# Second attention batch's value products in plain float32, a later landing time in the load planner, and conversion buffers reused for kept weight parts

## The chip, the cores and the metric

The kernel runs on one core of one Trainium2 chip. The metric is the device time of one execution in microseconds (us). Before the change three runs gave 1292.48, 1296.36 and 1309.52 us, a median of 1296.36 us.

## The reference

Attention over 4 batches of 12 heads, 448 positions and 64 values a head, with q and k normalised by their root mean square; then two feed-forward nets on the 1792 tokens (768 to 2048 to 768), the first with a squared ReLU, the second with a PReLU. All in float32.

```python
def _attn_ref(q, k, v, g_q, g_k):
    q_n, k_n = (rmsnorm(q, g_q), rmsnorm(k, g_k))
    scores = scale * np.matmul(q_n, k_n.transpose(0, 1, 3, 2))
    scores = scores - np.max(scores, axis=-1, keepdims=True)
    attn = np.exp(scores)
    attn = attn / (np.sum(attn, axis=-1, keepdims=True) + 1e-09)
    return np.matmul(attn, v).astype(np.float32)
...
    h = np.maximum(x @ w_in, 0.0)
    return (h * h @ w_out).astype(np.float32)
...
    h = x @ w_in
    g = np.maximum(h, 0.0) + alpha * np.minimum(h, 0.0)
    return (g @ w_out).astype(np.float32)
```

## The kernel before, in words

**Numbers in two parts.** Most products on TensorE are not done in plain float32 but in float32r, with each factor split into a high part (a rounded copy) and a low part (the remainder, `rest`, L259). One product of two split factors is three matmuls: high by low, high by high, low by high. The helper `copy` (L248) makes high parts on ScalarE, VectorE or GpSimd, `rest` low parts on VectorE or GpSimd.

**Stages.** `with_attention` (L422) holds the attention of all four batches and the first net (`mlp`, kind 0) of batches 0 and 1, one batch at a time. `without` (L826) then runs the first net of batches 2 and 3 together and the second net of all, two batches at a time.

**Attention.** A batch has six pairs of heads. For a pair, `spread` (L628) makes two matmuls on TensorE (L636) that bring the norms into the layout of q and k, and VectorE multiplies (L641); there are 12 such matmuls a batch, 48 in all, and their rows mark how far attention has come. `prep` (L663) splits the result into parts (tiles mv and st). `shift` (L679) computes rough scores (L685) of which VectorE takes the row maxima (L689); a transpose (L692), a negated copy (L695) and a small DMA (L697) bring them into mv. `head` (L699) computes the scores (L710) in four blocks of keys, ScalarE takes exponentials (L718), and the values are multiplied in. This last step has two forms. Where (batch, pair) is in `IN_PARTS` (L23), v is split into vhl, blocks have 128 keys (the last 64), ScalarE takes each exponential twice, once rounded into tile hl and once in full, VectorE makes the remainder (L744, a call of `rest`), and TensorE does 3 + 3 + 3 + 2 float32r matmuls a head (L753). Where it isn't, blocks have 112 keys, ScalarE writes one float32 exponential into tile pf, and TensorE does four float32 matmuls a head (L729), each of which the trace shows as two records. `norm` (L760) divides and splits the result into xs.

**Weights.** They come in parts (`weight`, L265): 32 of the first matrix of a net, of 384 KB, and 24 of the second, of 512 KB. In batch 0's net the first net's weights arrive as raw float64 words: a load into one of three raw tiles, ScalarE (L292) and four VectorE steps (L294, L297, L301, L304) that make float32 in one of three ws tiles, then a high part by ScalarE and a low part by GpSimd in one of three whl tiles, and a store of whl to DRAM ("kept"). I call these steps one conversion; there are 56 in this stage. Batch 1's net, and the first net in `without`, load kept parts straight into whl. The second net's weights are converted in `without` in the same way.

**Order.** All engines run lists that are fixed when the kernel is built. `Tasks.run` (L99) makes them: each piece of work is a task with an urgency, prices in us for the engines that may do it, and dependencies; the scheduler plays it through and emits the task that can start soonest, by urgency where several can. Buffers come from named pools, and a task that needs one gets the one that comes free first by the plan. A load is planned (L161 and L162) to cost its bytes at a rate (`load`, L209) one after another, with a latency ahead of it and one behind. All DMAs are issued in one list by SyncE (SP), in order; one that waits keeps back those behind it.

Of the kernel before, what the change touches and what calls it, by code (L numbers as in the profile page):

```python
# [19 lines left out]
DM, DFF = 768, 2048  # L20
KD, KF = DM // 128, DFF // 128

IN_PARTS = {(b, p) for b in (2, 3) for p in range(NP)} | {(1, 3), (1, 4), (1, 5)}  # L23
GROUPS = ((2, 4), (2, 4))
SPARE = (("mv", 2), ("st", 2))
NSEL = max(max(g) for g in GROUPS)
# [26 lines left out]
class Tasks:  # L53
# [45 lines left out]
    def run(self):  # L99
        ready = {e: [] for e in self.ends}  # L100

        def offer(t):
            for e in t.on:
                ready[e].append(t)

        for t in self.new:
            for d in (*t.deps, *t.behind):
                if d.start is None:
                    t.missing += 1
                    d.next.append(t)  # L110
        for t in self.new:
            if not t.missing:
                offer(t)
        left = len(self.new)
        self.new = []
        while left:
            best = None
            for e, tasks in ready.items():
                found, soonest = [], None
                for t in tasks:  # L120
                    s = self.ends[e] + (max(t.gap, self.gap[e]) if e in "AV" else 0)
                    s = max(s, self.port) if e in t.alone else s
                    for d in t.deps:
                        s = max(s, d.end + (0 if d.engine == e == "T" else self.WAIT[e]))
                    for d in t.behind:
                        s = max(s, d.start)
                    taken = []
                    for b in t.bufs:
                        if b.ap is None:
                            taken.append(self.slot(b, taken))  # L130
                            s = max(s, taken[-1][0] + self.WAIT[e]) if taken[-1] else None
                            if s is None:
                                break
                    if s is None:
                        continue
                    if len(t.on) > 1:
                        other = min(max(self.ends[o], s, self.port if o in t.alone else 0) + self.PRICE[o] * t.on[o]
                                    + 0.7 * sum(x.on[o] for x in ready[o] if x.urgency < t.urgency)
                                    for o in t.on if o != e)
                        if s + self.PRICE[e] * t.on[e] > other + 0.2:  # L140
                            continue
                    found.append((s, t.urgency, t))
                    soonest = s if soonest is None else min(soonest, s)
                if found:
                    s, _, t = min((x for x in found if x[0] <= soonest + 0.05), key=lambda x: x[1])
                    if best is None or s < best[0]:
                        best = (s, e, t)
            assert best, "no task can start"
            s, e, t = best
            for o in t.on:  # L150
                ready[o].remove(t)
            for b in t.bufs:
                if b.ap is None:
                    _, n, b.pool = self.slot(b)
                    slots = self.free[b.pool]
                    b.slot = slots.pop(next(i for i, x in enumerate(slots) if x[1] == n))
                    b.ap = b.slot[2]
            t.engine, t.start = e, s
            if e == "S" and t.on[e]:
                self.ends[e] = s + 0.06  # L160
                self.dma = max(self.dma, s + 1.3) + t.on[e]  # L161
                t.end = self.dma + 0.8  # L162
            else:
                t.end = self.ends[e] = s + t.on[e]
                self.gap[e] = t.gap
                if e in t.alone:
                    self.port = t.end
            t.emit(e)
            left -= 1
            for b in t.bufs:  # L170
                b.left -= 1
                b.until = max(b.until, t.end)
                self.release(b)
            for n in t.next:
                n.missing -= 1
                if not n.missing:
                    offer(n)
# [15 lines left out]
def dve(n):  # L193
    return 0.07 + 0.00104 * n
# [12 lines left out]


def load(nbytes):  # L209
    return nbytes / 350e3  # L210


MM = 0.202
# [3 lines left out]
def attention_relu2_mlp_prelu_mlp(ctx: ExitStack, tc: tile.TileContext, qkt, qk_tm, v, gb, alpha, ident, sel,  # L217
# [18 lines left out]
    kept = {id(w1): [Buf(dram.tile([128, 2, UP], F32, name=f"w1_{i}")) for i in range(2 * KF)],  # L236
            id(w2): [Buf(dram.tile([128, 2, DN], F32, name=f"w2_{i}")) for i in range(4 * KD)]}
    y_dram = [[Buf(dram.tile([128, S], F32, name=f"y{b}_{d}")) for d in range(KD)] for b in range(2)]
    for name, n, dt, size in (("raw", 3, U32, 2 * DN), ("ws", 3, F32, DN), ("whl", 3, F32R, 2 * DN)):
        pooled(const, name, n, [128, size], dt)  # L240

    only = {}

# [21 lines left out]
    def weight(u, w, i, source, urgency, after):  # L265

        n = w.shape[-1] // 2
        both = Buf(pool="whl")
        parts = [(both, 0), (both, 1)]

        def part(k):
            return both.ap[:, k * n:k * n + n]

        def pair():
            return both.ap[:, :2 * n].bitcast(F32).rearrange("p (k n) -> p k n", k=2)

        if source == "kept":
            k = kept[id(w)][i]
            add(urgency, {"S": load(1024 * n)}, dma(pair, lambda: k.ap), [k], parts, "wh")
            return both  # L280
        raw, f = Buf(pool="raw"), Buf(pool="ws")
        add(urgency, {"S": load(1024 * n)}, dma(lambda: raw.ap[:, :2 * n], lambda: w[i]), [], [raw], "raw", after)

        def half(k):
            return raw.ap[:, :2 * n].rearrange("p (n two) -> p n two", two=2)[:, :, k]

        def fu():
            return f.ap[:, :n].bitcast(U32)


        add(urgency, {"A": act(n)},
            lambda e: nc.scalar.activation(out=f.ap[:, :n], in_=half(1).bitcast(F32), func=ACTF.Abs), [raw], [f], "f")  # L292
        add(urgency, {"V": dve2(n)},
            lambda e: nc.vector.tensor_scalar(out=f.ap[:, :n], in0=f.ap[:, :n], scalar1=TINY, scalar2=None, op0=ALU.max),  # L294
            [], [f])
        add(urgency, {"V": dve2(n)},
            lambda e: nc.vector.tensor_scalar(out=fu(), in0=fu(), scalar1=0x07FFFFFF, scalar2=3,  # L297
                                              op0=ALU.bitwise_and, op1=ALU.logical_shift_left), [], [f])

        add(urgency, {"V": dve(n)},  # L300
            lambda e: nc.vector.scalar_tensor_tensor(out=fu(), in0=half(1), scalar=0xC0000000, in1=fu(),  # L301
                                                     op0=ALU.bitwise_and, op1=ALU.bitwise_or), [raw], [f])
        add(urgency, {"V": dve(n)},
            lambda e: nc.vector.scalar_tensor_tensor(out=fu(), in0=half(0), scalar=29, in1=fu(),  # L304
                                                     op0=ALU.logical_shift_right, op1=ALU.bitwise_or), [raw], [f])
        add(urgency, on("wh", A=act(n), V=dve2(n)), lambda e: copy(e, part(0), f.ap[:, :n]), [f], [(both, 0)], "wh")
        add(urgency, on("wl", P=pool2(n), V=dve(n)), lambda e: rest(e, part(1), f.ap[:, :n], part(0)),
            [f, (both, 0)], [(both, 1)], "wl")
        if source == "first":
            k = kept[id(w)][i]  # L310
            add(urgency, {"S": load(1024 * n)}, dma(lambda: k.ap, pair), parts, [k], "keep")
        return both

    stream = []
    for s1, more in (("first", 0), ("kept", 0), ("kept", 2)):
        stream += [(w1, i, s1) for i in range(2 * KF)] + [(w2, i, s1) for i in range(4 * KD)]
        for _ in range(more):
            stream += [(w3, i, "f64") for i in range(2 * KF)] + [(w4, i, "f64") for i in range(4 * KD)]
    made, cur = {}, [0]

    def prepare(u, urgency, after=None):
        if u < len(stream) and u not in made:
# [99 lines left out]
    def with_attention():  # L422
        with ExitStack() as es:
# [378 lines left out]
            def give(bank):  # L802
# [3 lines left out]
                    ts.free["m"].append((bank.slot[0], bank.slot[1], bank.ap.rearrange("p (t n) -> p t n", t=1)))  # L806
                add(-100, {"S": 0}, emit, [], [bank], None, first_scores[0, H - 1])

            setup()
            attention(0, 0, True)  # L810
            for _ in range(2):
# [2 lines left out]
                prepare(u, 95, first_scores[0, 7])  # L814
            only.update(wl="P", wh="A")
            mlp(0, (0,), hg, to_dram(1, [y_dram[0]]), 10000, 140, 2.6)
            attention(1, 200)
            mlp(0, (1,), hg, to_dram(1, [y_dram[1]]), 20000, 340, 5.2)
            attention(2, 400)
            attention(3, 600)  # L820
            for u in range(cur[0], cur[0] + 3):
                prepare(u, 5000)
                made[u].open = True
            ts.run()

    def without():  # L826
        with ExitStack() as es:
            q1 = es.enter_context(tc.tile_pool(name="q1", bufs=1))
            pp = es.enter_context(tc.tile_pool(name="pp2", bufs=1, space=PSUM))
            hg = fixed(q1, [128, 2, KF, 2, S], F32R, "hg2")  # L830
            pooled(q1, "rl", 3, [128, 2, S], F32)
            pooled(q1, "y", 2, [128, 2, S], F32)
            pooled(pp, "m", 4, [128, 2, 512], F32)
# [83 lines left out]
```

## Time and profile before

| what | value |
|---|---|
| median of three runs | 1296.36 us |
| the profiled execution, its own time | 1297.45 us |
| its span, first to last instruction | 1295.6 us |
| TensorE, VectorE, ScalarE, GpSimd busy | 1232.6, 800.8, 720.9, 373.5 us |
| mean granted clock of TensorE | 0.978 of full speed |
| start of the last stage's products (m from xs) | 590.87 us |

The page of the profile gives busy times of the engines over the whole span and in 40 slices of 32.4 us. The view of stretches gives them between two points in time, with the granted clock and the busy share of the DMA engines. The chain that ended last lists, in order of time, which piece of work or which transfer the end hung on. The timeline lists an engine's instructions with the idle time ahead of them and what ended it. PE is TensorE, PEld its weight loads, DVE VectorE, ACT ScalarE, POOL GpSimd, SP or SPq SyncE's list of DMAs.

### The profile page before, as it was taken

The page shows a single profiled execution, that of the slowest core. Times are in us where ns is not written, and L with a number is a line of the kernel's source. Part 1 is how long each engine was busy: PE and PEld are TensorE (multiplying, and loading weights), DVE is VectorE, ACT ScalarE, POOL GpSimd, SP SyncE. Part 2 cuts the span into 40 slices and gives each one's busy share as a digit, 9 for nine tenths or more (in the row PEclk, how much of TensorE's full clock was granted, in tenths as well). Part 3 has the DMA queues.
Part 4 walks back from the last instruction along what each step waited for, and adds up shares of the span by engine and source line. Part 5 has one row for each costly group of instructions (what it writes and reads, how often), then busy time and mean ns, then how long its engine had stood idle before and what let it go on. Part 6 is the DMA issues. An engine that isn't in the chain of part 4 may idle for free.

```text
span 1295.6 us, 16918 instructions
## 1 busy us (share of the span) xinstructions
PE 1232.6 (95%) x5790; PEld 1073.4 (83%) x5790; DVE 800.8 (62%) x1419; ACT 720.9 (56%) x1350; POOL 373.5 (29%) x354
## 2 busy tenths in 40 slices
PE   4997899797999899999999999999999999999998
PEld 2556677675888788888999999999999999999997
DVE  6688899999888688602111000487895548786550
ACT  4788689776699879823333000366653336664331
POOL 3245345535345525310000000222232222223221
PEclk7998999998999899999999999999999999999999
DMA  5136658788445544257333323233354333334330
GB/s 184 54 117 228 237 202 277 275 280 274 170 145 180 193 145 136 81 188 246 105 105 120 114 100 112 83 105 111 125 180 155 119 114 98 114 123 137 133 112 29
DMA packets 69014, 194.45 MB, mean 150 GB/s; under 512 B 8320, under 2 KB 14592, under 8 KB 68928
## 3 DMA queue, kind: packets, MB, share of 16 engines
q1 hardware_dynamic: 68928, 193.38, 45.1%
q8 instruction: 45, 0.74, 0.2%
q14 instruction: 41, 0.34, 0.1%
HBM read 159.84 MB, written 33.42 MB: 149 GB/s over the span
## 4 chain that ended last, share of the span: by engine, by line
PE 80%; DVE 10%; ACT 4%; DMA 3%; issue 2%; SPq 0%; POOL 0%; ACTq 0%; DVEq 0%
PE m L343 54%; PE bank L343 11%; PE bank L710 5%; PE pv L753 4%; PE pv L729 3%; PE bank L685 2%; DVE mc L689 1%; DVE ws L301 1%; DMA whl<-w 1%; DVE hl L259 1%; DVE ws L304 1%; DVE ws L294 1%; DMA tm<-in_qk_tm 1%; DMA raw<-in_w 1%; DVE ss L588 1%
## 5 line engine op out<-in xcount | busy, mean ns | idle before, releaser
L259 POOL TENSOR_TENSOR whl<-ws,whl 128x384 fp32r<-128x384 f32 (+2 forms) x169 | 204.9, 1215 | 683.4 <-ACT whl L251 405.2
L343 PE MATMUL m<-xs,whl 128*128 128x448 f32 x1728 | 350.8, 365 | 0.7 <-ACT rl L251 0.7
L343 PE MATMUL m<-hg,whl 128*128 128x448 f32 x1728 | 350.7, 365 | 0.0
L343 PEld LDWEIGHTS m<-xs,whl 128*128 128x128 f32 x1728 | 324.5, 188 | 26.7 <-ACT rl L251 1.1
L343 PEld LDWEIGHTS m<-hg,whl 128*128 128x128 f32 x1728 | 324.5, 188 | 25.7
L292 ACT ACTIVATE ws<-raw 128x384 f32<-128x384 f32 (+1 forms) x168 | 101.3, 603 | 133.5 <-POOL whl L259 112.3
L294 DVE TENSOR_SCALAR ws<-ws 128x384 f32<-128x384 f32 (+1 forms) x168 | 68.0, 409 | 142.6 <-ACT ws L292 142.4
L343 PE MATMUL bank<-xs,whl 128*128 128x448 f32 x576 | 142.4, 382 | 7.8 <-POOL xs L259 3.3
L251 ACT ACTIVATE whl<-ws 128x384 fp32r<-128x384 f32 (+1 forms) x167 | 94.4, 566 | 77.3 <-PE m L343 57.1
L343 PE MATMUL bank<-hg,whl 128*128 128x448 f32 x576 | 130.6, 369 | 2.2 <-DMA whl<-w 2.2
L343 PEld LDWEIGHTS bank<-xs,whl 128*128 128x128 f32 x576 | 111.5, 196 | 21.2 <-POOL xs L259 3.7
L343 PEld LDWEIGHTS bank<-hg,whl 128*128 128x128 f32 x576 | 108.9, 191 | 11.8 <-DMA whl<-w 2.6
L304 DVE SCALAR_TENSOR_TENSOR ws<-raw,ws 128x384 uint32<-128x384 uint32 (+1 forms) x168 | 116.3, 698 | 2.7
L689 DVE TENSOR_REDUCE mc<-bank 112x1 f32<-112x448 f32 x192 | 110.3, 615 | 11.4 <-PE bank L685 10.2
L259 DVE TENSOR_TENSOR hg<-m,hg 128x896 fp32r<-128x896 f32 x48 | 52.1, 1086 | 94.1 <-ACT hg L251 93.6
L301 DVE SCALAR_TENSOR_TENSOR ws<-raw,ws 128x384 uint32<-128x384 uint32 (+1 forms) x168 | 106.5, 639 | 3.7
L710 PE MATMUL bank<-mv,st 128*128 128x448 f32 (+2 forms) x352 | 102.2, 397 | 5.3 <-ACT mn L695 2.4
L259 DVE TENSOR_TENSOR hl<-bank,hl 128x448 fp32r<-128x448 f32 (+1 forms) x120 | 73.7, 618 | 32.6 <-ACT bank L718 31.5
L753 PE MATMUL pv<-hl,vhl 128*128 128x448 f32 x330 | 87.3, 374 | 1.3 <-DVE hl L259 1.3
L685 PE MATMUL bank<-st,mv 128*112 128x448 f32 x176 | 62.2, 411 | 22.5 <-DVE mc L689 7.8
L710 PEld LDWEIGHTS bank<-mv,st 128*128 128x128 f32 (+2 forms) x352 | 60.9, 182 | 24.9 <-DVE mc L689 6.3
L297 DVE TENSOR_SCALAR ws<-ws 128x384 uint32<-128x384 uint32 (+1 forms) x168 | 72.7, 439 | 3.6
(110 smaller groups left out, 1259.5 us busy)
## 6 DMA issues: line engine op xcount, KB each, us to landing
raw<-in_w SPq DMA_DIRECT2D x96, 384.0 KB
raw<-in_w SPq DMA_DIRECT2D x72, 512.0 KB
whl<-w SPq DMA_DIRECT2D x64, 384.0 KB
whl<-w SPq DMA_DIRECT2D x48, 512.0 KB
w<-whl SPq DMA_DIRECT2D x32, 384.0 KB
w<-whl SPq DMA_DIRECT2D x24, 512.0 KB
qk<-in_qkt SPq DMA_DIRECT2D x24, 448.0 KB
tm<-in_qk_tm SPq DMA_DIRECT2D x40, 224.0 KB
```

The lines of the kernel that those rows point to most:

```text
L251: nc.scalar.activation(out=o, in_=i, func=ACTF.Copy)
L259: (nc.gpsimd if e == "P" else nc.vector).tensor_tensor(out=o, in0=x, in1=hi, op=ALU.subtract)
L292: lambda e: nc.scalar.activation(out=f.ap[:, :n], in_=half(1).bitcast(F32), func=ACTF.Abs), [raw], [f], "f")
L294: lambda e: nc.vector.tensor_scalar(out=f.ap[:, :n], in0=f.ap[:, :n], scalar1=TINY, scalar2=None, op0=ALU.max),
L297: lambda e: nc.vector.tensor_scalar(out=fu(), in0=fu(), scalar1=0x07FFFFFF, scalar2=3, op0=ALU.bitwise_and, op1=ALU.logical_shift_left), [ ...
L301: lambda e: nc.vector.scalar_tensor_tensor(out=fu(), in0=half(1), scalar=0xC0000000, in1=fu(), op0=ALU.bitwise_and, op1=ALU.bitwise_or), [ ...
L304: lambda e: nc.vector.scalar_tensor_tensor(out=fu(), in0=half(0), scalar=29, in1=fu(), op0=ALU.logical_shift_right, op1=ALU.bitwise_or), [ ...
L343: nc.tensor.matmul(out=acc.ap[:, t, :S], lhsT=w.ap[:, part * n + 128 * kk:part * n + 128 * kk + 128], rhs=src(h, k0 + kk, t)[1](), start=( ...
L685: lambda e, t=t, pm=pm: nc.tensor.matmul(out=pm.ap[:CP, :S], lhsT=m.ap[:, 0, t * CP:(t + 1) * CP], rhs=s.ap[:, 0, :], start=True, stop=Tru ...
L689: lambda e, t=t, pm=pm: nc.vector.reduce_max(out=mc.ap[:, t:t + 1], in_=pm.ap[:CP, :S], axis=AX.X),
L710: nc.tensor.matmul(out=pa.ap[:keys, :S], lhsT=s.ap[:rows, k, c:c + keys], rhs=m.ap[:rows, k, :], start=(k == 0), stop=(k == 1))
L753: nc.tensor.matmul(out=o.ap[:, :S], lhsT=l, rhs=r, start=(n == 0 and x == 0), stop=(half and x == 1))
```

## The change

**What it does.** Three edits. (1) `IN_PARTS` loses pairs 3, 4 and 5 of batch 1, so that all of batch 1's value products are plain float32, as batch 0's are (the host lays out v by the same set). (2) The planner counts 2.0 us ahead of a load and 1.4 us behind it, where it counted 1.3 and 0.8, and a rate of 320 GB/s where it counted 350. (3) raw and ws are no longer allocated for the whole kernel. In `with_attention` they lie in a pool of their own, which is closed behind the last conversion of that stage (`no_more`); four more tiles of whl's size, named more, take its room and serve as further buffers for kept parts until that stage ends. `without` allocates raw and ws anew.

```diff
-IN_PARTS = {(b, p) for b in (2, 3) for p in range(NP)} | {(1, 3), (1, 4), (1, 5)}
+IN_PARTS = {(b, p) for b in (2, 3) for p in range(NP)}
...
             if e == "S" and t.on[e]:
                 self.ends[e] = s + 0.06
-                self.dma = max(self.dma, s + 1.3) + t.on[e]
-                t.end = self.dma + 0.8
+                self.dma = max(self.dma, s + 2.0) + t.on[e]
+                t.end = self.dma + 1.4
...
 def load(nbytes):
-    return nbytes / 350e3
+    return nbytes / 320e3
...
-    for name, n, dt, size in (("raw", 3, U32, 2 * DN), ("ws", 3, F32, DN), ("whl", 3, F32R, 2 * DN)):
-        pooled(const, name, n, [128, size], dt)
+    pooled(const, "whl", 3, [128, 2 * DN], F32R)
+
+    def converting(pool):
+
+        pooled(pool, "raw", 3, [128, 2 * DN], U32)
+        pooled(pool, "ws", 3, [128, DN], F32)
...
-        both = Buf(pool="whl")
+        both = Buf(pool=("whl", "more") if "more" in ts.free else "whl")
...
-        add(urgency, on("wl", P=pool2(n), V=dve(n)), lambda e: rest(e, part(1), f.ap[:, :n], part(0)),
+        converted[0] = add(urgency, on("wl", P=pool2(n), V=dve(n)), lambda e: rest(e, part(1), f.ap[:, :n], part(0)),
...
+            wp = es.enter_context(ExitStack())
+            converting(wp.enter_context(tc.tile_pool(name="wp", bufs=1)))
+
+            def no_more():
+
+                def emit(e):
+                    until = max(x[0] for n in ("raw", "ws") for x in ts.free[n])
+                    wp.close()
+                    pool = wp.enter_context(tc.tile_pool(name="wq", bufs=1))
+                    ts.free["more"] += [(until, i, pool.tile([128, 2 * DN], F32R, name=f"more{i}")) for i in range(4)]
+
+                add(-100, {"S": 0}, emit, [], [], None, converted[0])
+
+            ts.pool("more", [])
             setup()
             attention(0, 0, True)
...
             mlp(0, (0,), hg, to_dram(1, [y_dram[0]]), 10000, 140, 2.6)
+            no_more()
             attention(1, 200)
...
             attention(3, 600)
+            del ts.free["more"]
             for u in range(cur[0], cur[0] + 3):
                 prepare(u, 5000)
                 made[u].open = True
+            ts.pool("more", [])
             ts.run()
+            del ts.free["more"]
...
             hg = fixed(q1, [128, 2, KF, 2, S], F32R, "hg2")
+            converting(q1)
```

**What it does to the order.** Since the scheduler plays all of this through, the order changes on every engine, from the first microseconds on. How many MLP products (L343) stand ahead of a spread matmul on TensorE, and how many conversions (L304) ahead of that spread's product on VectorE (L641):

| spread matmul | 13th (batch 1) | 17th | 21st | 25th (batch 2) | 29th | 33rd |
|---|---|---|---|---|---|---|
| MLP products before | 15 | 117 | 195 | 456 | 552 | 621 |
| MLP products now | 15 | 108 | 204 | 279 | 420 | 558 |
| conversions before | 5 | 17 | 26 | 48 | 56 | 56 |
| conversions now | 4 | 16 | 27 | 37 | 48 | 56 |

In the changed kernel the line numbers are 4 higher. VectorE where the values of pair 3 of batch 1 are multiplied, before: hg is a remainder of the net's hidden layer, hl one of the exponentials, mc the maxima of rough scores, ws a conversion.

```order
L259 TENSOR_TENSOR hl_175<-bank_150,hl_175 128x448
L689 TENSOR_REDUCE mc_185<-bank_154 112x1
L259 TENSOR_TENSOR mv_159<-bank_152,mv_159 64x448
L689 TENSOR_REDUCE mc_185<-bank_150 112x1
L689 TENSOR_REDUCE mc_185<-bank_154 112x1
L259 TENSOR_TENSOR hg<-bank_153,hg 128x448
L259 TENSOR_TENSOR hl_176<-bank_151,hl_176 128x448
L294 TENSOR_SCALAR ws_138<-ws_138 128x384
L294 TENSOR_SCALAR ws_136<-ws_136 128x384
```

And there now:

```order
L263 TENSOR_TENSOR hg<-bank_149,hg 128x448
L693 TENSOR_REDUCE mc_180<-bank_148 112x1
L305 SCALAR_TENSOR_TENSOR ws_195<-raw_193,ws_195 128x384
L298 TENSOR_SCALAR ws_196<-ws_196 128x384
L308 SCALAR_TENSOR_TENSOR ws_195<-raw_193,ws_195 128x384
L301 TENSOR_SCALAR ws_196<-ws_196 128x384
L693 TENSOR_REDUCE mc_180<-bank_145 112x1
L305 SCALAR_TENSOR_TENSOR ws_196<-raw_192,ws_196 128x384
L693 TENSOR_REDUCE mc_180<-bank_146 112x1
```

The hl remainders are gone, and conversions and maxima stand closer to each other.

SP around the loads of kept parts 18 to 22 of the first matrix (w1_18 to w1_22), in the stretch with batches 2 and 3, before: whl0 to whl2 are the three buffers, qk, tm and v attention's inputs.

```order
L262 DMA whl1_140<-w1_18_83 128x768
L262 DMA tm0_171<-in_qk_tm 112x512
L262 DMA tm1_172<-in_qk_tm 112x512
L262 DMA whl2_141<-w1_19_84 128x768
L262 DMA tm0_171<-in_qk_tm 112x512
L262 DMA whl0_139<-w1_20_85 128x768
L262 DMA qk0_166<-in_qkt 128x896
L262 DMA qk1_167<-in_qkt 128x896
L262 DMA whl1_140<-w1_21_86 128x768
L262 DMA tm1_172<-in_qk_tm 112x512
L262 DMA whl2_141<-w1_22_87 128x768
```

And now:

```order
L266 DMA more3_2924<-w1_18_83 128x768
L266 DMA qk1_161<-in_qkt 128x896
L266 DMA tm0_165<-in_qk_tm 112x512
L266 DMA v0_162<-in_v 128x768
L266 DMA whl2_135<-w1_19_84 128x768
L266 DMA tm1_166<-in_qk_tm 112x512
L266 DMA whl0_133<-w1_20_85 128x768
L266 DMA whl1_134<-w1_21_86 128x768
L266 DMA more0_2921<-w1_22_87 128x768
```

The same parts go through seven buffers in turn, so that a buffer's load waits for the part seven places back to be used, where it waited for the one three places back.

## Rows read from the trace of the kernel before

**Rows 1.** The page: busy time, then tenths in 40 slices.
```profile
PE 1232.6 (95%) x5790; PEld 1073.4 (83%) x5790; DVE 800.8 (62%) x1419; ACT 720.9 (56%) x1350; POOL 373.5 (29%) x354
...
PE   4997899797999899999999999999999999999998
...
DVE  6688899999888688602111000487895548786550
...
PEclk7998999998999899999999999999999999999999
```

**Rows 2.** Stretches: length, busy PE, PEld, DVE, ACT, POOL (instructions), clock, DMA share, GB/s.
```profile
300.00:325.00 25.00, 15.66 (x63) 12.50 (x62) 22.98 (x42) 14.72 (x28) 14.56 (x14) 0.80 0.75 262
...
442.50:451.84 9.34, 6.09 (x17) 5.39 (x18) 3.71 (x7) 5.35 (x12) 3.29 (x4) 0.63 0.63 215
...
556.00:590.87 34.87, 31.98 (x159) 29.05 (x157) 0.62 (x1) 5.09 (x9) 3.46 (x3) 1.00 0.63 208
590.87:1295.60 704.73, 700.68 (x3456) 649.02 (x3456) 340.02 (x552) 274.75 (x416) 130.47 (x112) 1.00 0.36 119
...
110.14:345.16 235.02, 203.75 (x886) 164.08 (x886) 217.96 (x424) 180.32 (x374) 104.36 (x90) 0.94 0.72 247
345.16:590.87 245.71, 238.58 (x1154) 208.30 (x1154) 162.03 (x285) 184.84 (x394) 94.51 (x96) 0.99 0.47 154
```

**Rows 3.** The chain that ended last: start us, us, what.
```profile
73.91 2.31 PE pv L729 x6
...
438.81 6.90 DMA whl<-w
...
568.48 6.96 DMA whl<-w
...
587.59 2.70 DMA whl<-w
590.87 700.70 PE m L343 x3456
```

**Rows 4.** TensorE's timeline: start us, us, instruction, [idle before, what ended it].
```profile
110.14 1.05 PE L636 MATMUL bank<-rhl,selg 128*128 128x448 f32 x4 [1.78 <-DVE rhl L259]
...
163.56 0.82 PE L636 MATMUL bank<-rhl,selg 128*128 128x448 f32 x2 [0.18 <-DVE rhl L259]
...
198.44 0.93 PE L636 MATMUL bank<-rhl,selg 128*128 128x448 f32 x2
...
317.51 0.69 PE L685 MATMUL bank<-st,mv 128*112 128x448 f32 x1 [6.24 <-ACT ws L292]
...
345.16 0.65 PE L636 MATMUL bank<-rhl,selg 128*128 128x448 f32 x2 [0.40 <-DVE rhl L259]
...
445.75 3.73 PE L343 MATMUL bank<-xs,whl 128*128 128x448 f32 x9 [3.26 <-DMA whl<-w]
...
575.49 0.68 PE L343 MATMUL bank<-hg,whl 128*128 128x448 f32 x2 [2.21 <-DMA whl<-w]
```

**Rows 5.** VectorE's groups, 110.14 to 345.16: count, busy us, mean ns, idle before.
```profile
L689 DVE TENSOR_REDUCE mc<-bank 112x1 f32<-112x448 f32 x64 | 37.4, 614 | 3.4 <-PE bank L685 3.0
L304 DVE SCALAR_TENSOR_TENSOR ws<-raw,ws 128x384 uint32<-128x384 uint32 (+1 forms) x52 | 31.9, 630 | 0.2
L301 DVE SCALAR_TENSOR_TENSOR ws<-raw,ws 128x384 uint32<-128x384 uint32 (+1 forms) x51 | 31.6, 637 | 0.1
L297 DVE TENSOR_SCALAR ws<-ws 128x384 uint32<-128x384 uint32 (+1 forms) x51 | 23.6, 481 | 0.1
L294 DVE TENSOR_SCALAR ws<-ws 128x384 f32<-128x384 f32 (+1 forms) x51 | 21.1, 429 | 4.5 <-ACT ws L292 4.2
L259 DVE TENSOR_TENSOR hl<-bank,hl 128x448 fp32r<-128x448 f32 (+1 forms) x30 | 17.9, 614 | 0.8 <-ACT bank L718 0.6
...
L259 DVE TENSOR_TENSOR st<-bank,st 64x448 fp32r<-64x448 f32 x16 | 10.0, 622 | 0.6 <-ACT st L251 0.2
...
L259 DVE TENSOR_TENSOR vhl<-v,vhl 128x768 fp32r<-128x768 f32 x1 | 2.0, 2047 | 0.0
```

More of the change, by code (lines that the diff above doesn't have):

```diff
@@ L318, in attention_relu2_mlp_prelu_mlp @@
             stream += [(w3, i, "f64") for i in range(2 * KF)] + [(w4, i, "f64") for i in range(4 * KD)]
-    made, cur = {}, [0]
+    made, cur, converted = {}, [0], [None]
     def prepare(u, urgency, after=None):
```

## The prediction

> **What bounds the kernel now.** I read the page's slices first [rows 1]: TensorE is busy for 95% of the span, so only its gaps and its slow-clock stretches can be had. From slice 19 on it stands at 9 with the granted clock at 9; before that it falls to 6 and 7, with the clock down to 7 and 8. The stretches [rows 2] put the border at 590.87 us: behind it 700.7 us of 704.7 are busy, and the chain [rows 3] holds nothing there but one piece of 700.70 us, 3456 products. That gives the price of a product that I use below, 700.70 / 3456 = 0.203 us. The change alters nothing that this stage computes, so its cost stays.
>
> The time to be had lies in the 590.87 us ahead. I cut it where the spread matmuls stand [rows 4], which mark how far attention has come: the 13th (first of batch 1) at 110.14 and the 29th (batch 2, second pair) at 345.16, just after the last weight conversion. In the first stretch, 110.14 to 345.16, VectorE is busy for 217.96 of 235.02 us (93%) and TensorE for 203.75 [rows 2]; what TensorE waits for there is VectorE work, as in front of the 317.51 us row, where it stood for 6.24 us [rows 4]. (The row names ScalarE's conversion; VectorE was doing that conversion's next steps.) So VectorE sets the pace. In the second stretch, to 590.87, VectorE is down to 162 of 246 us and TensorE at 239: TensorE sets it. What it loses there are mostly waits for kept weights: 3.26 us at 445.75, with a mean granted clock of 0.63 around it (part of that stretch at the lower of its two levels, 1.2 and 2.4 GHz), and 2.21 us at 575.49 [rows 2, 4].
>
> **Pairs 3 to 5 of batch 1 in float32.** Each of six heads loses 11 products (3+3+3+2) and gains four float32 products. Six records of L729 take 2.31 us in the chain [rows 3]; two records are one product, so 0.77 us. TensorE: 24 x 0.77 - 66 x 0.203 = +5.1 us. VectorE loses 24 subtractions of hl at some 0.61 us, ScalarE 24 exponentials, GpSimd and VectorE the split of three v tiles. These pairs lie in the first stretch (of its 30 hl rows on VectorE [rows 5], 24 are theirs and 6 batch 2's).
>
> A rule of the Trainium skill bears on the price: FP8 and Floating Point Precision, TensorE Precision Notes, counts four passes for true FP32. At 0.203 us a pass that would be 0.81 us and +6.1 in all; the row's 0.77 is taken here.
>
> What this does to the first stretch I work out from the orders. By VectorE's order the last conversion stands ahead of the 29th spread before, and ahead of the 33rd now: batch 1's attention has become cheaper, and the scheduler puts more attention, two pairs of batch 2, among the conversions. So I compare VectorE's work from the 13th spread to the 29th before with that from the 13th to the 33rd now, at its mean durations [rows 5]. Before it sums to 242 us, which with overlaps filled 218. Now: one conversion more (four steps, 0.63 + 0.64 + 0.48 + 0.43 = +2.2), 16 maxima (16 x 0.614 = +9.8), 12 spread products and mv and st remainders (12 x 0.62, st's row, = +7.5), 8 hl remainders fewer (-4.9), a v split fewer (-2.0), the small ones together -1.2: 253 us. At the same overlap and the same 93% that takes 253/242 x 235.0 = 246.0 us: the 33rd spread comes at 356.2.
>
> TensorE's work left behind that point now: 594 MLP products, 144 of scores, 64 of maxima, 206 of values, 16 spreads, all at 0.203, and 17 transposes of 0.1: some 209 us. Before, behind the 29th spread: 600, 176, 80, 250, 20 and 21, some 230 us, done in 245.7 us, a rate of 0.938. At that rate 209 us take 223.2, and the stretch ends at 579.4 instead of 590.9: **-11.5 us**, with the 5.1 us of float32 inside. ScalarE covers this: it is busy for 180 of 235 us in the first stretch and 185 of 246 in the second [rows 2], and has no more rows per pair than before.
>
> **Four more buffers for kept parts, and loads planned later.** The new tiles lie where raw and ws were, and their first loads stand behind the last conversion, as SP's order shows. From then on seven parts can be on their way or in store. Before, three: a load of 384 KB took 6.90 us in the chain, and at 568.48 one of 512 KB 6.96 [rows 3], while TensorE uses a part up in 9 x 0.203 = 1.8 or 12 x 0.203 = 2.4 us. Three parts in store cover 5.5 to 7.3 us, seven 12.8 to 17. Price: around 445.75 TensorE did 18 products, 3.6 us, in 9.34; in the last 34.87 us it did 159 by the records, 32.3 us [rows 2]. So 5.7 + 2.6 = 8.3 us are there to be had; nothing, at the other end, if SP still issues late. SP takes its DMAs in order, and loads of qk, tm and v that wait for VectorE stand among those of parts; with seven in store such a block is covered. I take **-6**.
>
> The planner counted 1.3 + 1.1 + 0.8 = 3.2 us for a 384 KB load and now counts 2.0 + 1.2 + 1.4 = 4.6. The rows show 6.90 and 2.70 [rows 3]; 4.6 lies between them. The Trainium skill speaks against this part: in DMA: Bandwidth & Descriptors, Anatomy of one DMA, a fit (for GpSimd's path) gives 2.0 us plus the bytes at 436 GB/s, 2.9 us here. By it the old plan was right and this edit is worth nothing; 6.90 us disagrees, 2.70 agrees. I give the plan no term of its own.
>
> In the third stage raw and ws are allocated anew, over tiles of attention's stage, so the first raw load waits in SP's queue for the last product on hg. Behind it stand loads of kept parts, which wait for TensorE to free a buffer anyway, with three parts loaded: 0 us. If that cover failed, one part's wait of 2.70 us [rows 3] would be the cost.
>
> **A held-back part.** Between the 17th and the 25th spread the new order leaves TensorE 171 MLP products where 339 stood, with the float32 products of batch 1 in between: 90 us of TensorE's work beside 99 of VectorE's, which at 0.90 overlap and 93% would take 96 us. Both engines close to full at once: from the 17th to the 21st before, 33.2 us of TensorE's work were done in 34.9 (163.56 to 198.44 [rows 4]), 0.95, but over the whole first stretch 184 in 235, 0.78. By the first nothing is lost, by the second 90/0.78 - 96 = 19. I take **+4**, nearer the first, since there too the work was balanced.
>
> **Sum.** -11.5 - 6 + 4 = -13.5. The profiled execution took 1297.45 us, 1295.6 of it span; 1.1 more than the median of 1296.36. So 1284 for it, and 1283 for a median.
>
> **The rivals.** *Nothing to gain (0.17).* The relief is eaten by the denser first stretch (+12 instead of +4) and the parts land no sooner, since SP's order is fixed and its blocks remain: the four buffers then don't do what they were put there for. -11.5 + 12 + 0: 1297. For it: ScalarE and DMA are also 72 to 77% busy there [rows 2]. Against it: neither is the one waited for longest.
>
> *The idle time of VectorE goes too (0.12).* Of its 17 us idle in the first stretch, half goes because raw parts are asked for earlier, and both waits for parts vanish: -11.5 - 8.3 - 8.5, or 1268. For it: 4.5 us of it are waits for ScalarE's first step [rows 5], which itself waits for raw loads. Against it: VectorE's waits are spread over many causes.
>
> *TensorE starves between the 17th and 25th spread (0.13).* With half the MLP products, heads wait for their own chain (maxima, transpose, a small DMA, exponentials), and TensorE's clock goes down with its gaps, as in the slice from 300 to 325 us: 15.66 of 25 busy at a clock of 0.80 [rows 2]. At a rate of 0.70 the 90 us take 129, 33 more than 96: -11.5 - 6 + 33 = +15.5, or 1312. It decides from a rate of 0.79 down, where the 17.5 us are used up. For it: the first stretch had just 0.78. Against it: VectorE was what held it down.
>
> **How the numbers follow.** The forecast, 1272 to 1293, has 0.58. The range of 1268 to 1299 takes in the second rival at its own figure and the first whole, and leaves out most of the third. A measurement of this kernel tells about 2%, 26 us, from no change: faster than 1270.4 is most of the second rival (0.10), slower than 1322 the end of the third (0.04), the rest, 0.86, lies within.
>
> **What would show it.** Right: the 33rd spread near 356 us with the conversions just done, VectorE at 93% up to there; the piece of 3456 products beginning near 577; no wait for whl or more over 1 us in TensorE's rows of the second stretch. Wrong: TensorE's busy time from the 17th to the 25th spread under 80% with VectorE under 90% (the third rival); a start of the last stage before 565 (the second); waits for kept parts as long as before (the first).

## The result and the profile after

The changed kernel takes 1275.38 us (median of four runs, 1274.14 to 1275.94) where the kernel before took 1294.43 (median of its four, with one more run than ahead of the prediction). The ratio is 0.9865, with a 95% interval of 0.9841 to 0.9889: faster by 1.35%. The forecast was 1283, with a range of 1268 to 1299. Single late executions pull a ratio, so below the median stands beside it where the two differ.

The stretches of the changed kernel, cut at the same marks as in [rows 2]: the first, its part from the 17th to the 25th spread matmul, the second, the last stage. Columns as there.

```profile
111.18:352.44 241.26, 223.28 (x973) 175.29 (x974) 228.38 (x446) 196.37 (x411) 129.10 (x101) 0.97 0.72 247
352.44:567.41 214.97, 213.67 (x1050) 188.64 (x1048) 136.10 (x240) 158.73 (x336) 79.88 (x81) 1.00 0.54 171
156.81:252.40 95.59, 93.07 (x380) 66.17 (x380) 89.51 (x177) 84.48 (x181) 53.09 (x44) 1.00 0.71 238
567.41:1272.40 704.99, 700.87 (x3456) 649.72 (x3456) 340.71 (x552) 274.17 (x416) 129.85 (x112) 1.00 0.38 119
```

TensorE's timeline at the marks, which answer to [rows 4]:

```profile
111.18 1.08 PE L640 MATMUL bank<-rhl,selg 128*128 128x448 f32 x4 [2.50 <-DVE rhl L263]
...
252.40 1.34 PE L640 MATMUL bank<-rhl,selg 128*128 128x448 f32 x4
...
352.44 0.57 PE L640 MATMUL bank<-rhl,selg 128*128 128x448 f32 x2
...
567.41 8.78 PE L347 MATMUL m<-xs,whl 128*128 128x448 f32 x42 [0.68 <-ACT rl L255]
```

The chain that ended last, at the border that [rows 3] show at 590.87:

```profile
527.04 39.70 PE bank L347 x195
...
567.41 700.88 PE m L347 x3456
```

The 33rd spread stands at 352.44 us (forecast: 356), the last stage begins at 567.41 (forecast: 577) instead of 590.87 and costs the same 705 us, and ahead of it 195 products run in one piece of 39.70 us (0.204 us each) where the chain of [rows 3] passes through two loads of kept parts. The two executions profiled are 23 us apart; the medians, 19. The profiled execution of before is 3 us above its median, and its stretch of 235.02 us [rows 2] was shorter in others, as the runs below show.

### The profile page after: what moved, and what is told of

Same layout as the page of the kernel before. It is cut to its first block, busy times and chain, and to the rows that moved or that the text cites. A ratio compares the mean times of both kernels' runs of the same rounds, so it can differ in the third digit from the quotient of the medians.

```text
span 1272.4 us, 16814 instructions
## 1 busy us (share of the span) xinstructions
PE 1227.0 (96%) x5772; PEld 1065.8 (84%) x5772; DVE 781.9 (61%) x1390; ACT 708.1 (56%) x1326; POOL 387.0 (30%) x353
## 4 chain that ended last, share of the span: by engine, by line
PE 79%; DVE 10%; ACT 6%; issue 2%; POOL 1%; DMA 1%; SPq 0%; ACTq 0%; POOLq 0%; DVEq 0%
PE m L347 55%; PE bank L347 11%; PE bank L714 4%; PE pv L757 3%; PE pv L733 3%; PE bank L689 2%; DVE mc L693 2%; DVE ws L305 1%; DVE ws L308 1%; DMA tm<-in_qk_tm 1%; DVE bank L645 1%; DVE ws L298 1%; DVE ss L592 1%; ACT mv L255 1%; DVE st L263 1%
## 5 line engine op out<-in xcount | busy, mean ns | idle before, releaser
L263 POOL TENSOR_TENSOR whl<-ws,whl 128x384 fp32r<-128x384 f32 (+2 forms) x169 | 209.5, 1242 | 668.1 <-ACT whl L255 375.4
L305 DVE SCALAR_TENSOR_TENSOR ws<-raw,ws 128x384 uint32<-128x384 uint32 (+1 forms) x168 | 105.0, 628 | 3.9
L347 PE MATMUL bank<-xs,whl 128*128 128x448 f32 x405 | 100.5, 380 | 5.5 <-POOL xs L263 5.2
L714 PE MATMUL bank<-mv,st 128*112 128x448 f32 (+2 forms) x352 | 98.4, 390 | 0.7 <-ACT pf L722 0.5
L347 PE MATMUL bank<-hg,whl 128*128 128x448 f32 x420 | 93.4, 367 | 0.0
L347 PEld LDWEIGHTS bank<-xs,whl 128*128 128x128 f32 x405 | 77.5, 194 | 15.9 <-POOL xs L263 5.6
L347 PEld LDWEIGHTS bank<-hg,whl 128*128 128x128 f32 x420 | 79.2, 190 | 6.4
L301 DVE TENSOR_SCALAR ws<-ws 128x384 uint32<-128x384 uint32 (+1 forms) x168 | 73.7, 443 | 3.8
L263 DVE TENSOR_TENSOR hl<-bank,hl 128x448 fp32r<-128x448 f32 (+1 forms) x96 | 59.1, 620 | 27.3 <-ACT bank L722 24.3
L714 PEld LDWEIGHTS bank<-mv,st 128*112 128x112 f32 (+2 forms) x352 | 60.1, 178 | 18.6 <-issue 4.4
L689 PE MATMUL bank<-st,mv 128*112 128x448 f32 x176 | 62.9, 414 | 12.1 <-DVE st L263 9.4
L757 PE MATMUL pv<-hl,vhl 128*128 128x448 f32 x264 | 69.0, 370 | 1.9 <-DVE hl L263 1.6
```

Of the source, the lines that this page charges most:

```text
L263: (nc.gpsimd if e == "P" else nc.vector).tensor_tensor(out=o, in0=x, in1=hi, op=ALU.subtract)
L347: nc.tensor.matmul(out=acc.ap[:, t, :S], lhsT=w.ap[:, part * n + 128 * kk:part * n + 128 * kk + 128], rhs=src(h, k0 + kk, t)[1](), start=( ...
L689: lambda e, t=t, pm=pm: nc.tensor.matmul(out=pm.ap[:CP, :S], lhsT=m.ap[:, 0, t * CP:(t + 1) * CP], rhs=s.ap[:, 0, :], start=True, stop=Tru ...
L714: nc.tensor.matmul(out=pa.ap[:keys, :S], lhsT=s.ap[:rows, k, c:c + keys], rhs=m.ap[:rows, k, :], start=(k == 0), stop=(k == 1))
L757: nc.tensor.matmul(out=o.ap[:, :S], lhsT=l, rhs=r, start=(n == 0 and x == 0), stop=(half and x == 1))
```

## The experiments

All ratios are to the kernel before on the same chip. The three edits were tried alone and in pairs, then the pace of the first stretch.

**Edit 1 alone.**

```diff
-IN_PARTS = {(b, p) for b in (2, 3) for p in range(NP)} | {(1, 3), (1, 4), (1, 5)}
+IN_PARTS = {(b, p) for b in (2, 3) for p in range(NP)}
```

> Edit 1 alone (batch 1's values all in plain float32; planner and buffers as before). Theory, VectorE's relief: the 33rd spread comes near 356 us as in the forecast, the waits for kept parts stay (3 us near 445, 2 us near 575), the whole is 9 to 12 us shorter than before (ratio 0.991 to 0.993). Rival, the later planned landing is what shortens the first stretch: within 3 us of before. Rival, TensorE starves between the 17th and 25th spread: slower than before by 5 us or more.

Measured: 0.9967 (0.9941 to 0.9993), 4 us; 6 by the medians. The 33rd spread came at 364.69 us, not at 356, and in the stretch up to it ScalarE waited 12.9 us for raw parts. The view of stretches, 13th to 33rd spread, then the view of waits there (who <- for whom: us in total, times, longest):

```profile
110.81:364.69 253.88, 225.80 (x971) 178.07 (x971) 231.37 (x444) 194.54 (x403) 122.78 (x107) 0.96 0.71 238
```

```profile
ACT ws L292 <- DMA raw<-in_w: 12.9, 11, 4.3
```

So a third to a half of the forecast's 11.5 us came out. The waits for kept parts stayed, but none over 0.7 us: that part of the expectation fell.

**Edit 2 alone.**

```diff
-                self.dma = max(self.dma, s + 1.3) + t.on[e]
-                t.end = self.dma + 0.8
+                self.dma = max(self.dma, s + 2.0) + t.on[e]
+                t.end = self.dma + 1.4
...
-    return nbytes / 350e3
+    return nbytes / 320e3
```

> Edit 2 alone (loads planned to land later). Theory: no term of its own, within 3 us of before (ratio 0.998 to 1.002), waits for raw parts in the first stretch about as long as before. Rival, the plan does most of it: 8 us shorter or more (ratio under 0.994), with TensorE's idle time in the first stretch down by that.

Measured: 0.995 (0.9925 to 0.9974), 6.5 us: as much as edit 1 within the intervals, and between the theory's figure and the rival's. My theory that this edit has no term of its own fell here. The same row of the waits:

```profile
ACT ws L292 <- DMA raw<-in_w: 0.5, 1, 0.5
```

With the old plan ScalarE waited for raw parts ten or eleven times in the first stretch; with the new one, once for 0.5 us. Yet the stretch itself is not shorter for it. Here it is, 13th to 29th spread, in this run, and in two whose order on every engine is that of before up to there, edit 3 alone and the shorter maxima further down, with their waits for raw parts:

```profile
113.15:343.65 230.50, 203.71 (x893) 165.10 (x894) 219.24 (x426) 181.88 (x378) 110.20 (x88) 0.95 0.75 253
```

```profile
110.22:340.81 230.59, 202.17 (x886) 163.48 (x886) 218.10 (x424) 180.50 (x374) 103.26 (x90) 0.95 0.75 251
...
108.90:339.52 230.62, 202.45 (x885) 163.78 (x886) 211.35 (x424) 179.84 (x374) 103.21 (x90) 0.94 0.75 251
```

```profile
ACT ws L296 <- DMA raw<-in_w: 9.3, 11, 2.1
...
ACT ws L292 <- DMA raw<-in_w: 9.5, 11, 1.9
```

What is shorter in this trace is the second stretch, 239.05 us against 243.49 in the run of the shorter maxima (which has neither the plan nor the buffers), and there TensorE's waits for kept parts. First edit 2, then that run:

```profile
343.65:582.70 239.05, 235.20 (x1147) 206.27 (x1145) 161.65 (x284) 187.00 (x397) 93.80 (x96) 0.99 0.51 159
...
339.52:583.01 243.49, 238.16 (x1154) 207.24 (x1154) 162.16 (x285) 184.84 (x394) 94.75 (x96) 0.99 0.50 156
```

```profile
PE bank L343 <- DMA whl<-w: 1.2, 2, 0.8
...
PE bank L343 <- DMA whl<-w: 3.5, 2, 3.0
```

Ahead of the 13th spread edit 2 is 4 us later than that run (113.15 and 108.90), so the two reach the last stage together (582.70 and 583.01); where the 6.5 us between the medians lie, these traces don't show.

**Edit 3 alone** (the pools wp, wq and more as in the change, IN_PARTS and the planner as before).

> Edit 3 alone (four more buffers for kept parts once the conversions are done; the order up to there is that of before). Theory: the waits for whl near 445 and 575 us are gone, 4 to 8 us shorter (ratio 0.994 to 0.997), the first stretch unchanged. Rival, SP still issues late because of its order: waits of 2 us or more remain, within 2 us of before.

Measured: 1.0012 (0.9973 to 1.0051), no change that can be told. Its profiled execution shows both sides. The second stretch is down to 238.80 us (before: 245.71; the run of the shorter maxima: 243.49), with no wait for whl in it:

```profile
340.81:579.61 238.80, 236.82 (x1154) 206.12 (x1155) 162.14 (x285) 184.43 (x393) 94.81 (x97) 1.00 0.50 159
```

But the last stage, which the forecast gave 0 us, costs 707.8 us (from 579.61 to the span's end at 1287.4) instead of 704.7. SP's list after the border, and TensorE:

```profile
584.19 0.71 SPq L266 DMA_DIRECT2D whl<-w  x1
590.49 0.33 SPq L266 DMA_DIRECT2D raw<-in_w  x1
590.87 0.91 SPq L266 DMA_DIRECT2D y<-y  x2
591.81 0.43 SPq L266 DMA_DIRECT2D whl<-w  x1
```

```profile
597.22 3.11 PE L347 MATMUL m<-xs,whl 128*128 128x448 f32 x14 [1.79 <-DMA whl<-w]
```

After the load at 584.19 SP stands until the next raw load goes at 590.49, and the kept part behind it goes at 591.81 only: TensorE waits for a part. In the whole change this did not happen, and the stage took 705.0; with edits 1 and 3 it took 705.7. This trace is of an execution of 1289.18 us, where the median is 1295.41, so the stage's 3 us alone don't explain why nothing was gained.

**The pairs.** Edits 1 and 2, without the buffers:

> Edits 1 and 2 without the four buffers. Alone, edit 1 gave 0.997, edit 2 0.995, edit 3 1.001, the whole 0.9865: some 8 us come from two edits together. Theory, plain float32 frees VectorE and that pays only where raw parts land in time: edits 1 and 2 carry nearly all, ratio 0.986 to 0.990, first stretch (13th to 33rd spread) near 241 us as in the whole change. Rival, the buffers carry the longer tail of products that edit 1 leaves: ratio 0.992 to 0.995.

Measured: 0.9902 (0.9884 to 0.9919), 12.7 us, just short of the theory's band. ScalarE waited for raw parts once in the first stretch, for 0.4 us. Edits 1 and 3, with the old plan:

> Edits 1 and 3 with the planner as before. Theory as above: as edit 1 alone, ratio 0.995 to 0.998, first stretch near 254 us, raw loads in its chain for 9 us or more. Rival, the buffers: ratio under 0.992.

Measured: 0.9972 (0.9941 to 1.0003), 6 us by the medians, inside the theory's band. First stretch, 13th to 33rd spread, and its waits for raw parts:

```profile
109.59:362.96 253.37, 229.18 (x970) 180.40 (x971) 229.76 (x444) 193.66 (x403) 129.96 (x107) 0.95 0.72 244
```

```profile
ACT ws L296 <- DMA raw<-in_w: 15.5, 10, 3.0
```

Edits 2 and 3, without the float32 products:

> Edits 2 and 3, batch 1's last three pairs in parts as before. Theory as above: as edit 2 alone, ratio 0.993 to 0.997, no wait for whl over 1 us in the second stretch. Rival, edits 2 and 3 are the pair that gains: ratio under 0.990.

Measured: 0.9915 (0.9899 to 0.9931), 11 us, outside the theory's band and short of the rival's.

What follows, in thousandths of the time before: float32 takes off 3 alone and 5 beside the other two (0.9915 to 0.9865); the plan 5 alone and 11 beside the other two (0.9972 to 0.9865); the buffers nothing that can be told alone, and 4 beside the other two (0.9902 to 0.9865, where the two intervals just overlap). By the medians it is 5, 5 and nothing alone, and 6, 9 and 5 beside the others. The three alone add up to 7 of the whole's 13.5 by the ratios, to some 10 of 14 by the medians; the rest needs them together.

The traces show where. With the old plan edit 1 shortens the way from the 13th to the 33rd spread by 12 us (from 266.22 in edit 3 alone to 253.88), with the new plan by 23 (from 266.18 in edit 2 alone to 243.05 in edits 1 and 2):

```profile
110.22:376.44 266.22, 237.05 (x1054) 193.34 (x1055) 245.97 (x472) 210.38 (x438) 119.52 (x107) 0.96 0.73 243
...
113.15:379.33 266.18, 239.39 (x1070) 196.50 (x1070) 247.01 (x474) 214.63 (x448) 126.83 (x105) 0.96 0.72 241
...
111.45:354.50 243.05, 224.54 (x973) 176.18 (x974) 229.15 (x446) 196.55 (x411) 126.47 (x101) 0.96 0.71 245
```

Part of that comes back behind the mark, where edit 1 leaves more products (203.4 us from the 33rd spread to the last stage in edit 2 alone, 220.6 in edits 1 and 2). The buffers shorten the second stretch beside edits 1 and 2, from 220.6 to 215.0:

```profile
354.50:575.13 220.63, 216.15 (x1049) 189.33 (x1047) 137.22 (x239) 157.79 (x335) 82.32 (x83) 0.99 0.51 166
```

**More of edit 1.**

```diff
-IN_PARTS = {(b, p) for b in (2, 3) for p in range(NP)}
+IN_PARTS = {(b, p) for b in (2, 3) for p in range(NP)} - {(2, 0), (2, 1)}
```

> The whole change, and pairs 0 and 1 of batch 2 in plain float32 too: 16 x 0.77 - 44 x 0.203 = +3.4 us on TensorE, 16 hl remainders fewer on VectorE (-9.8 us of its work), all ahead of the last conversion. Theory, VectorE still sets the pace there: 3 to 6 us shorter than the change (ratio to before 0.982 to 0.984). Rival, VectorE has enough room by now and TensorE pays: 2 to 5 us longer than the change (ratio 0.988 to 0.990).

Measured: 0.9883 (0.9853 to 0.9913): not shorter than the change, whose interval it overlaps, so the theory fell. The first stretch took 239.1 us, 2 less, the second 220.5, 5.6 more.

**Is it VectorE that sets the pace?** Less work on VectorE with every engine's order as in the kernel before:

```diff
-                            lambda e, t=t, pm=pm: nc.vector.reduce_max(out=mc.ap[:, t:t + 1], in_=pm.ap[:CP, :S], axis=AX.X),
+                            lambda e, t=t, pm=pm: nc.vector.reduce_max(out=mc.ap[:, t:t + 1], in_=pm.ap[:CP, :S // 2 if b == 1 else S], axis=AX.X),
```

> The kernel before, its order unchanged on every engine, but batch 1's 48 row maxima of the rough scores (first stretch) are taken over half of the keys: this leaves out half of that work on VectorE, some 48 x 0.23 = 11 us by its durations, 10 us with overlaps. Theory, VectorE paces the first stretch: 7 to 11 us shorter, all of it between the 13th and the 29th spread. Rival, that stretch is paced by SP's order, the raw loads or ScalarE: under 3 us.

Measured: 1.0002 (0.9981 to 1.0022), although the maxima did become shorter, 383 ns each for [rows 5]'s 614:

```profile
L689 DVE TENSOR_REDUCE mc<-bank 112x1 f32<-112x224 f32 x48 | 17.2, 383 | 3.7 <-PE bank L685 3.3
```

Its first stretch is shown under edit 2: VectorE had 6.8 us less to do than in edit 3 alone (211.35 for 218.10), and the stretch took the same 230.6 us. The same on the changed kernel, and beside it the changed kernel once more:

> The changed kernel, its order unchanged, with batch 1's 48 row maxima over half of the keys (that half of the maxima's work is left out): some 11 us off VectorE's work in the first stretch. The same edit on the kernel before changed nothing (1.0002). Theory A, it was the raw loads landing late that hid it, and VectorE paces the stretch where they land in time: 7 to 10 us shorter than the changed kernel. Theory B, VectorE alone isn't the pace, since TensorE beside it is nearly full too (92%): within 3 us of the changed kernel.

> The changed kernel once more, beside the other three on one chip: ratio near 0.9865, 1275 us.

Measured: 0.9854 (0.9839 to 0.9869), and the changed kernel 0.9862 (0.9844 to 0.9881): theory B's time, not A's. VectorE has 8 us less to do than in that run (221 for 229) and the stretch is 2.7 us shorter (240.3 for 243.0). Then less work on TensorE:

```diff
+        parts_of = ((0, 1), (0, 0), (1, 0))[1 if slots == (0,) else 0:]
...
-                    for part, h in ((0, 1), (0, 0), (1, 0)):
+                    for part, h in parts_of:
...
-                                             stop=(last and kk == nk - 1 and j == 2))
+                                             stop=(last and kk == nk - 1 and j == len(parts_of) - 1))
```

> The changed kernel, its order unchanged, with two instead of three matmuls for each product of batch 0's first net: the low part of the activations is left out, 192 matmuls of 0.203 us, 39 us off TensorE's work, nearly all in the first stretch (13th to 33rd spread, 241 us). VectorE paces it: the stretch stays within 4 us. TensorE paces it: 30 us shorter or more. Theory B, both hold each other, and TensorE's share of the pace is the larger one: 10 to 25 us shorter.

Measured: 0.985 (0.9835 to 0.9865), 1.3 us shorter than the changed kernel by the medians. The first stretch, 13th to 33rd spread, of the changed kernel's second run, of the shorter maxima, and of the fewer products:

```profile
111.08:354.05 242.97, 224.08 (x974) 175.58 (x974) 229.28 (x446) 196.69 (x411) 127.10 (x101) 0.96 0.72 245
```

```profile
110.19:350.48 240.29, 223.55 (x974) 176.50 (x975) 221.29 (x446) 196.50 (x411) 125.86 (x101) 0.96 0.74 249
```

```profile
110.72:352.38 241.66, 201.98 (x792) 143.24 (x793) 229.61 (x446) 196.59 (x410) 129.27 (x101) 0.93 0.72 246
```

There are 182 products fewer in the stretch by the records than in the changed kernel's second run, some 37 us at 0.203 us each; TensorE's busy time fell by 22 us only, with the mean granted clock down from 0.96 to 0.93, and the stretch is 1.3 us shorter, with VectorE at 95%. TensorE's amount of work alone doesn't set the pace there, in spite of its 224 busy us of 243. Theory B of this run, in which TensorE's share of the pace was the larger, fell. That VectorE as the fullest engine sets it agrees with this run, but 8 us off VectorE brought 3 at most. The chain that ended last points at two paths of nearly the same length: added up over this stretch, its pieces are 89 us of VectorE and 89 of TensorE in the changed kernel's second run, 70 and 107 with the shorter maxima, 129 and 32 with the fewer products. It passes to the other engine as soon as one is relieved. Less work on both at once was not tried, nor less on ScalarE, busy for 196 us there, so what sets the pace stays open.

**Still later.** Latencies of 2.6 and 2.0 us and a rate of 290 GB/s:

```diff
-                self.dma = max(self.dma, s + 2.0) + t.on[e]
-                t.end = self.dma + 1.4
+                self.dma = max(self.dma, s + 2.6) + t.on[e]
+                t.end = self.dma + 2.0
...
-    return nbytes / 320e3
+    return nbytes / 290e3
```

> The changed kernel with loads planned to land later still (2.6 and 2.0 us, 290 GB/s; 5.9 us for a 384 KB load). Theory, the gain of edit 2 was ScalarE's waits for raw parts in the first stretch, 9 to 15 us of which 0.5 are left: nothing more to have, within 3 us of the changed kernel. Rival, margins are still too small: 4 us shorter or more.

Measured: 0.9967 (0.9927 to 1.0007), 13 us longer than the changed kernel: neither theory nor rival. The first stretch grew to 256.0 us and VectorE's busy time in it by as much:

```profile
111.42:367.41 255.99, 228.05 (x972) 178.49 (x973) 243.82 (x452) 194.83 (x408) 119.05 (x99) 0.95 0.70 238
```

GpSimd has 10 us less there (119 for 129), VectorE six instructions more (452 for 446); most of VectorE's 15 us are longer instructions (last section). Such a plan is not a margin that can be widened at will; it makes another order.

No version that does the whole work beat the change.

## Why the prediction was right, and where not

*The last stage stays.* Right: 705.0 us for 704.7. But its cover (loads of kept parts "wait for TensorE to free a buffer anyway") is not safe, as edit 3 alone showed with 3 us.

*The first stretch ends at 356, the second shrinks to 209 us of TensorE's work at a rate of 0.938: -11.5.* The sum held: edits 1 and 2 together took off 12.7 us, and the mark stood at 354.5 with them. The attribution failed. I booked all of it on the float32 products, "at the same overlap and the same 93%" of VectorE; alone they gave 4 to 6 us, and the 33rd spread came 8.5 us late. The step that failed is "I give the plan no term of its own": 6.5 us alone, 12 to 14 beside the other two. I had weighed it on single loads of kept parts (6.90 and 2.70 us) and looked neither at how often ScalarE's first step of a conversion waits for its raw part, ten times before, 9.5 us in all, nor at what a raw load takes. Both rows were to be had; of the groups, [rows 5] have only an echo, 4.2 us of VectorE waiting for that step (the prediction's 4.5 is all of that row's idle time). A raw load of 384 KB in before's chain:

```profile
133.50 5.57 DMA raw<-in_w
```

The Trainium skill's fit (DMA: Bandwidth & Descriptors, Anatomy of one DMA), which is for GpSimd's path while these loads go through SyncE's list, makes an estimate of 2.9 us for a load of this size. The row's 5.57 us disagrees; the old plan counted 3.2, the new one 4.6.

Why the plan pays is only in part shown. Beside edit 1 the waits for raw parts go from 12.9 and 15.5 us to 0.4 and none, and the first stretch gets 10.8 and 12.1 us shorter. But in edit 2 alone the same waits went and that stretch stayed at 230.5 us, VectorE's own waits for that step of ScalarE were only 4.2 and 3.7 us in the two runs with the old plan, and a new plan changes the order of everything; no run changed the landing with the order held.

Part of the agreement is luck. The forecast scaled the 235.0 us of the one execution profiled; from the 230.6 us of two other runs in the same order its own ratio, 253 by 242, gives 241.1, and 241.3 were measured. (Its first look was off too: ahead of slice 15 TensorE's digits fall to 7 and 8, and to 4 in the first slice, not to 6; nothing was worked out from that.)

*Four more buffers: -6 of the 8.3 to be had.* Right in size beside the new plan: 4.8 us by the ratios, 5.7 in the second stretch, and 5.5 there in edits 2 and 3 against edit 2 alone. Alone, nothing that can be told.

*A held-back +4.* Wrong: it should have been 0. From the 17th to the 25th spread the stretch took 95.6 us, the 96 of VectorE's work alone, with TensorE busy for 93.1 and at full clock. The run with fewer products agrees that there was room on that engine, busy as it reads: there this stretch took 96.3 us with nearly 60 of its 380 matmuls gone.

*VectorE sets the pace of the first stretch.* Not shown. TensorE's amount alone doesn't; VectorE stands at 91 to 95% in every version; but halving maxima brought 0 to 3 us of 7 to 8. The forecast's arithmetic, which turned VectorE's work into time at a fixed share, came out at the right mark without its reason being shown.

*The whole.* The last stage began 10 us ahead of the forecast's 577: 4 for the held-back part, 4 for the mark at 352 instead of 356, 2 for the second stretch.

*The rivals.* Starving did not happen (0.97 from the 17th to the 25th). The first rival fell: the waits for kept parts went, and the relief was not eaten. The second (1268, with a start of the last stage before 565) came close: 1275 lies half-way between it and the forecast. It named raw parts asked for earlier, and those waits did go; what that gave is open, as said above.

## What to carry to other kernels

Before an engine's relief is turned into time, count in the view of waits how often the steps that feed it wait for a transfer: here the same relief shortened its stretch by 12 us under the old landing times and by 23 under the new. A scheduler's assumed landing time is an edit with a price of its own, in both directions (6.5 us off alone, 13 us back when set later still). But a wait that goes is not yet time won: compare the stretch, and in more than one execution, since here one and the same order took 235.0 and 230.6 us. When several edits go in together, try them in pairs, since here a third to a half of the gain belonged to none of them alone. And an engine that reads as 92% busy may still have room: taking 182 products out of its stretch made that 1.3 us shorter.

## What the runs showed of the hardware that was not expected

Some of VectorE's instructions on SBUF operands take more than twice as long when they begin beside one of GpSimd's. In the run with loads planned still later, conversion steps (L305, a median of 682 ns from 200 us on) took 1.80 and up to 2.32 us. VectorE's timeline, the second row two steps in one piece, then GpSimd's:

```profile
248.47 1.80 DVE L305 SCALAR_TENSOR_TENSOR ws<-raw,ws 128x512 uint32<-128x512 uint32 x1
...
274.04 2.92 DVE L305 SCALAR_TENSOR_TENSOR ws<-raw,ws 128x512 uint32<-128x512 uint32 x2
```

```profile
248.02 1.70 POOL L263 TENSOR_TENSOR whl<-ws,whl 128x512 fp32r<-128x512 f32 x1 [0.29 <-ACT whl L255]
249.67 1.61 POOL L783 TENSOR_TENSOR d<-d,r 128x448 f32<-128x448 f32 x1
...
273.79 2.02 POOL L263 TENSOR_TENSOR vhl<-v,vhl 128x768 fp32r<-128x768 f32 x1
```

The long steps lie over GpSimd instructions with two SBUF operands. In that run the 24 steps of 512 columns averaged 940 ns, in the changed kernel 708. Of these 48 steps, the 32 that began while GpSimd was between instructions took 693 ns at most; of the 16 that began inside a GpSimd instruction, seven took 0.78 to 2.32 us and nine were no longer than the others. Steps with one SBUF operand grew too (L301 at 512 columns: 582 ns on average for 479). That the two engines hold each other up is read from the overlap; no run took GpSimd's work away, and why nine of the sixteen were not held up stays open.
